# A new precomputed instruction order and engine table for a fused attention and two-MLP kernel

## The chip, the cores and the metric

The kernel runs on one NeuronCore of one Trainium2 chip. The metric is the device time of one execution in microseconds (us). The engines are named as in the profile: PE (TensorE matmul), PEld (TensorE weight load, which overlaps PE), DVE (VectorE), ACT (ScalarE), POOL (GpSimd), SP (SyncE, which issues nearly all the DMAs).

## The reference, cut to what matters

Local attention with block summaries (2 batches, 8 heads, 768 positions, head size 64), and then two MLPs of 512 to 2048 to 512 on the 1536 tokens, all in float32:

```
k_sum = k.reshape(B, H, nb, 32, D).max(axis=3);  v_sum = v.reshape(B, H, nb, 32, D).mean(axis=3)
scores = concat(where(|i-j| < 16, q k^T / 8, -1e9), q k_sum^T / 8 + log 32)
x = softmax(scores) @ concat(v, v_sum)                  # to [1536, 512]
h = x @ w_in1
x = (P(h) / (Q(h) + 1e-6)) @ w_out1    # P cubic, Q = 1 + |b0||h| + |b1|h^2
h = x @ w_in2
out = (h * cos(h)) @ w_out2
```

The weights arrive as 64-bit floats, two 32-bit words for each value.

## The kernel before

Every matrix product is made of float32r matmuls on a high and a low part of each operand (three products: high by high, high by low, low by high). So every weight tile and every activation tile is converted or copied to a high part (`split`, line 757, on ACT, DVE or POOL; the profile shows it at the copy helper's lines L320 for ACT, L325 for DVE and L322 for POOL) and a low part is subtracted from it (`split`, line 759, on POOL or DVE; the profile shows L760). Weights are first rebuilt from their 64-bit form by three integer operations on DVE (`to_f32`, L743, L747, L751).

Attention works on 12 blocks of 128 tokens: scores (`sp`, L624), the mask with a running minimum (L639, DVE), the exponential with its sum (L643, ACT), the sum made safe and inverted (L648 on ACT or L649 on DVE, and L653 on DVE), the scaling of the probabilities (L656, POOL or DVE), their transpose (`ptp`, L670), the product with v (`avp`, L717), and then the high part of x (L320 or L325) and its low part (`xL`, L728, DVE). The first MLP's units follow behind as soon as their tokens are there: `h` (L847), the rational function (L996 to L1024 over ACT, DVE and POOL), and the second product into four PSUM banks (`acc`, L1089). A unit is one slice of 128 of the 2048 hidden columns and one tile of 512 tokens. When the token tile changes, a bank is copied out to SBUF (line 1114, "spill") and the next tile's partial sum is copied into it (line 1098, "reload"); both are copies on ACT (L320) or DVE (L325). The second MLP is made the same way for its first four slices and with a seven-product scheme (L945) for the rest.

Nothing of the order is decided on the chip. `Plan.op` records 2,989 operations with the engines on which each may run and a cost for the planner; `Plan.order` takes them in the order of a table, `ORDER`, which also holds one engine for each operation. The table was made beforehand by a search with replays of a cost model. What the chip runs is one queue for each engine, in that order, and semaphores between the engines. A cost that is of the class `Shared` marks an operation for which the planner reckons with the SBUF port that DVE and POOL share; the class is a float, and nothing on the chip reads it.

`coefficients` (lines 377 to 396) loads the MLP's a and b and makes the scalar sqrt-like coefficient of b from them: on DVE L384, L390, L392 and L395, on ACT L382, L387 and L389, all on 128x1 values.

Of the kernel before, what the change touches and what calls it, by code (L numbers as in the profile page):

```python
# [53 lines left out]


ORDER = (
    "c-rk*+pk>LUH;bkt+nr$*?Z5-p8Ms@nKN^IE<P9EVmq;2J4q7<D>1EO43s7$GBk-2QC9`EC_s_&La0FWfvReu5<;SVAX"
    "X54fd^h%At6-pAM}AI;FVX_ZN?`NLPFw=vo+_OJ!`M^yM5p9TWj0MV}D2}(ex3MEImnQz`3`C4*>*sI48c15oTRr`pyL"
    "P=ohc0o`}Ktt2wLpdrYLQ1S6Vbkclin>ka`K`YAr-UgLs?;8v9a7kDI(mnjeUJ~#v6BfPx;A0_R*6y9W9Wn}_<ke79k3"
    "A8hoHt=&%oYpU7|B)hkHVPpK@-G?op2Lf;?OwV0lrn<rH-7!%rB{|$aN*7Z-@kozvGv)@2f=sdTZi)-=fG!&@dmc`F78"  # L60
    "d2@9ki6<Hnio_y7Lv_ID>=$9VQ9<Bi$3W*g%_98V5^`NQ$}-r)lrjPAaCIoW^3e+lP)XZO&1{s?CemfQPx<xdy?{LIc<"
    "9XWq+zm}Koeg2K;?$5U_K08HoJR3Kg4=2N`SBA|SJA=#3e)GK8x{7jEmlxaZad|vy4KJ3h=H3DN)tOtJ0!6fF=Hq$Z+4"
    "xNPc$|-m7W&OzmbW&Mwr0ylI=)pbP+S|12IbY_@(X?sd82(Ui;mJe6_V%nlg4foU;mmsvmL#jytlX>Ch;%D(!aMcJ=n%"
    "8li=HTcE|f?XX6)kx4$~Zv;L!7x9}`~^vcA4S5C{f8?x(NYUFPwzE{_h&We4XQlGX%64~$f==H2aUOM_Pp`ia&@{>oop"
    "A^lM-l431LCWL@&6|mo6pE*_OB7rne?kxQI5`}=M(;P^N4?)Fvy{KOZ23vryUe|}wq&}o8F04kZEw=%R{xKwza!`#Mq3"
    "|%-mK~|Ugxi&?pJ8--ow9ruK8uO^1b)o-9~n_m}duz-E4E#z~WyPi}YV7S&E+xk@nyCam;!MM;!#WTRoutPyenAl-18<"
    "aR(v?5zg_b4SrU!dG}`V8F=~DO^F+G@r=auGKJt6v;g7PfrLkCf<c_&kfFxD1oyEGCUKFD6FL$I`49}-65{WKCf|=3u="
    "g=`A3uJKj~;)N-UQ+w0)N#Guc~=o@zS4rx4(ypm-Qr)eqVGG9nvCt898g{CW(KKCvAik+XJ3PBfwN3ewTU?g(|cryy_6"
    "jn`#KvDHshoJBMD>LkI1k3%?5d4OHH^^iq#^C7&e;*As)_pfCTyXQGIus3u}8$^q+n3~V>a61GGn!x9_8G)TtdAV~&ME"
    "IM7aESPy!=y{FIOCTFDDuFU+kRPQaV|+6Zp8Sn2FNuDwRj6)^d7QB@VFCMv4hsW>xr+6!$}zb^5qJl_DxSvSdQNzi$3x"  # L70
    "xu{t@cuf3<rSau3Tk=xHKe@B|k^r4ktV2!qO#JM~h^6q_;?@kOCRqdGe9L#otW+YhkM6+D!UpTdZ34igr$)+mldKRkyJ"
    "bWnS=;G&E{VIxp>%UCKg+fg)#lpskT6Ob6B0d-@FqNgH6Mff)pc^L3C@p(i)33(-cfYSFfkG_|Z5U7=Od4H<lP{^hI0e"
    "!RA=igUo;JfWbyN#XsZ!;g$uVX&@qY1=FSAj$XF!m602(f`Lim!YNJo$r!_vk)X#o7829x9b>2vXA5V?AA+`;f|o@;9b"
    "<c$*Xx(B!w2I)AxhQl4RXc1Q6w?kg&WtOF0%WwUy^kOl7Nij?OwijP2Dj@~ZY@lkqcDuY7BqS@XabVIQJ^eYJ2*i=7?u"
    "{@b;Ts+l;o+cYIg=`X+U}O9=M=uMzKf#Y7o3X3_KgYoH(ED47I{Zh`3jX?I;TQhc7ugSePyB`Kim>%(;imXFoNtJ7f{<"
    "heelDROMQ!S|!Xf8@&x_jI)U7q2sup|{GpOF!i{E)WMl|;kGz!Hf|5uozVdo1Z?r%L{<b94d?$Uz?rJx3hSE*0iARf$b"
    "x52J^Uu1H6g^6tROeWZQdWI2i1?PF2d3{wk)|iW>Y_jS3G&?TvR3mNh-l(79AibI)LD*0TrO2r*5eif+Xh5b+RP0S+L6"
    "_A-pCy&Y778cwv)Wg+8phKqibj(zrm}`Fk}F;<qVugrPaGXpdDzZF1k0p2QnvhT2i}qmi}-k;QtWo3x{s{aiqi|}I8GV"
    "~9`@qb(DRXcaWnLWVc-p!*Opxwp(&a#ma6bK30smMzaMj&AQ*AxG0CEuDU~iF>N7v}Bi>{|z|Inr8B;s=oclMpr{)c=u"
    "%WmbU11CAu;VsoY<e`AvXYA3dmX<quQ$83&$5lyvdLL7>=qlWj`R9f+{~)Dm*Oa@o4YZ>f(2zBh;2Vh@^PYCXo4tagD7"  # L80
    "O(B)A;oQglJVhZa0h$)?(}kEwA)2T21lre|1)Su_tQ(&Y;RuMdwE68l7zBJkJvf*v8~EKb-^O^v$fgi7gDab?rnm$LL_"
    ">Ma&tn#kEpseDm}pACcOW*CX*e9+AeAq0tzlAbU1&b?7y3z4xBUQ#uX$*nxa4B0e>??s-^(HVCFDQcwy&9Wuh6g0{_r<"
    "_tG647=nLZu$?_{2Mq9CBC5&DnWNf^AOKNr;WuOzi}NCB%HxjXI$AB_+MyMaZ)B)%J0ziL?|ISk4IPL6Y(Py%>t<%OJo"
    "!Y5H*wk!rtIkcw_y15sKnwxcBiMghsOBCQBFL#`lBn?v^DAo-xnc+J8V3x2m*l_-=DHGXprBxynzByTAN2_A-n0BEY7k"
    "4gxo-TT4kivaYEg-5|AO&8?TCPq^9zoM$fuAy5qR;vZa?A$kS^{`;-oB?kq$8JMnI}$h(fP2q#Zw5y4I^$^dc)uxFrzD"
    "0dhj$J6E@F{JN^9d8`BT~r@P(a`<O^j;P1;Z~vhfCZvE(loH_HK6FevFtDlrg6dW<lP62t{>sBO_>O7NBNL`rS@ez!Xg"
    "mDsDc7)n_*Wf>H$<DeB((l4c_N-xq`5{Nm%nc|b@6AcsxB-KPk*sLf=?junfUlgkFd~~_eLL~#>C2uK`wxP61?C8kVQ?"
    ";e|Y%H)fJVSCxVxjs+j0C3&Tq$2SZ-{m?FPfPsv_{T&GUahBc^CyEsHKpy?x@p79f~S|&vPCkVTz3rRA}l5?fa4oQB!+"
    "JEy^mM)<q_Hj0VM7sE!i8r#5D_!FcKbuC@ghtKJU<V=69v0Kn;Wdi^&S`(I6E|Kl>o{x98~UZ>aTb$Xp%r`PFqdi}q;g"
    "t<tlcVK2e`cA!WGWDAg7wTTUPN}b49jWvv3H4ge^chSLn0n5*dUsUc%os5y!1awDS9YKWlm#=QR@m?6M(7#Jo?fUXkTw"  # L90
    "asR1Mh`X0m%|*K!@0j**#F$}c0gN`TBi+6x`49aWF@B(CS_IITb8Iwa%FB*#c6Njhi!$0TpEQa@Zf(u4Z-#`-n2P<HgN"
    "4ph(9#V}#$<ZUHjhPa8uM6Jj4I%V6`gqRD%xHHpD9Kzh_IQ4gOOEes2nCqD)J7KNs$7H>j{K$qwcoL_{6&g=+0qbA7s&"
    "<<BYZ6f78g+{#)5&7JhD_-UJ4_k$EbU!r8+yJjAvY8<9&{oaKIcl;jjbvsi~$p;FcY`~T_bMcBa6GC8+Q?6Rdrh-H*8="
    "sAUOsa-nt~Y1wjL-254p4;%x$E+K+kduoN+9tf4g%Z7}5A5pzR~45-|83oPwjMRi8jkfEgo*|Gs^KrN``T1J1k{<u<`8"
    "HQ6XXj@Ef-8u@<iH})gCToUiTr4KEqO>N7amL}WKe>DzGTFE-Z&$wc8sVI*b9quvw}jbp*$R>ik?W?i-t{`uEvq8)l?m"
    "=ZGnL?Q34SU?z8c`JN!TY-;kH4I#Avs0t!<`j_of!khKZY#ZE#|%4zw~OOfuXOebonMHW97*)zWswP1E#NBy6`B5}BM$"
    "X2SB@rfOZe8o36Bqk+zn9AK;JTaz~N6*o=Qt$B+KtvR=9YSWu8dP_oKsim2^2FhUSu(!^Q{JSQ!?zk<W3xsRoaX6Tw@F"
    "yJ5;qVi*;0AN2Ij&c=GfuWrt0bA#FlMpiPDEF&;8IzoWRr6E3)f{%NL<sqXt)zr7vGvarfgOvUFmGLYxb|C&q=Z)xGji"
    "lLM>&sn+!NMNw}4t1j0S!YadQOxZTn8|JLbeYk6|0krO;;ML3?BqFOhcR_d`18g86c`-&Yf<`|ufOgJsH_Gz_unPdc3E"
    "4b?yZh2#qXSS8rkXeTuj_|JYS6>{1*-9m}jIPB4w%>$pP|&LPS1Fh!SYz;s9305bG*-ntsU~n`;H!JAb>)f3xTah?WhW"  # L100
    "LgzOuL4m~g`IIvC-K20>3It|W`BDlofGkSn9^O0&`GdaT0MBb;a@Dei1$7pylT+oo<4XX|b1gnYw|h$jN-;CQl;*va<P"
# [1205 lines left out]
```

## Time and profile before

| | |
|---|---|
| median of 3 runs (lowest, highest) | 611.24 us (610.29, 613.06) |
| the profiled execution's own time | 610.86 us |
| its span, first to last instruction | 609.1 us |
| PE, PEld busy | 589.6 us, 498.1 us |
| DVE, ACT, POOL busy | 563.3 us, 426.9 us, 313.6 us |

The profile is of one execution. Its span is 1.76 us under that execution's time and 2.1 us under the median of the runs. Busy times are unions: two instructions of an engine that overlap in the pipeline count once there, while a mean duration of one instruction counts each in full.

### The profile page before, as it was taken

How to read it: one execution, taken by the hardware profiler on the slowest of the kernel's cores; microseconds unless marked ns; L12 is line 12 of the kernel's file. 1: busy time of each engine (PE TensorE's matmuls, PEld its weight loads, DVE VectorE, ACT ScalarE, POOL GpSimd, SP SyncE). 2: the span in 40 equal slices, each digit the busy share in tenths (PEclk: the TensorE clock that was granted, in tenths of full speed). 3: DMA queues.
4: the chain of work that ended last, by engine and by line, in shares of the span. 5: the costliest groups of instructions: out<-in, count | busy, mean ns of one | idle time of the engine just before them, and what ended most of it. 6: DMA issues, size and time to landing. Idle time of an engine off the chain costs nothing.

```text
span 609.1 us, 10750 instructions
## 1 busy us (share of the span) xinstructions
PE 589.6 (97%) x3843; PEld 498.1 (82%) x3843; DVE 563.3 (92%) x1108; ACT 426.9 (70%) x930; POOL 313.6 (51%) x301
## 2 busy tenths in 40 slices
...
GB/s 259 230 238 179 214 186 179 32 0 2 104 49 56 69 70 103 104 35 70 69 70 34 36 69 70 35 70 9 95 105 1 110 63 105 53 19 0 53 36 121
DMA packets 68861, 51.84 MB, mean 85 GB/s; under 512 B 37304, under 2 KB 63160, under 8 KB 68808
## 3 DMA queue, kind: packets, MB, share of 16 engines
...
q8 instruction: 30, 0.49, 0.3%
...
## 4 chain that ended last, share of the span: by engine, by line
PE 54%; DVE 36%; issue 4%; ACT 3%; POOL 1%; DMA 1%; DVEq 0%; ACTq 0%; POOLq 0%
PE acc L1089 25%; PE h L945 15%; PE h L847 9%; DVE h L1021 4%; DVE tu L1018 3%; DVE f L747 3%; DVE te L1024 3%; DVE f L751 3%; DVE te L1008 3%; DVE f L743 3%; DVE te L1010 3%; DVE sc L639 2%; DVE gl L760 2%; PE ktp L461 1%; PE avp L717 1%
## 5 line engine op out<-in xcount | busy, mean ns | idle before, releaser
L1089 PE MATMUL acc<-gh,w 128*128 128x512 f32 (+1 forms) x416 | 123.1, 378 | 1.9 <-ACT acc L320 1.2
L1089 PE MATMUL acc<-w,gh 128*128 128x512 f32 x382 | 119.2, 393 | 0.8 <-ACT room L320 0.8
L847 PE MATMUL h<-xH,w 128*128 128x512 f32 (+1 forms) x352 | 111.4, 374 | 0.7 <-DVE big L493 0.7
L1089 PEld LDWEIGHTS acc<-gh,w 128*128 128x128 f32 x416 | 75.2, 188 | 19.2 <-ACT acc L320 2.6
L760 POOL TENSOR_TENSOR gl<-te,gh 128x512 fp32r<-128x512 f32 (+1 forms) x48 | 63.3, 1320 | 52.3 <-DVE gh L325 27.3
L760 POOL TENSOR_TENSOR w<-f,w 128x512 fp32r<-128x512 f32 x48 | 66.7, 1391 | 39.6 <-ACT w L320 27.1
L1006 POOL TENSOR_TENSOR tu<-tu,tf 128x512 f32<-128x512 f32 (+1 forms) x46 | 59.6, 1296 | 40.7 <-ACT tf L998 38.9
L1089 PE MATMUL acc<-gl,w 128*128 128x512 f32 (+1 forms) x208 | 78.0, 375 | 0.0
L1089 PEld LDWEIGHTS acc<-w,gh 128*128 128x128 f32 x382 | 67.3, 189 | 11.3 <-ACT room L320 1.2
L847 PEld LDWEIGHTS h<-xH,w 128*128 128x128 f32 x352 | 64.5, 188 | 12.8 <-DVE big L493 0.9
L1089 PE MATMUL acc<-w,gl 128*128 128x512 f32 x191 | 74.3, 389 | 0.0
L847 PE MATMUL h<-xL,w 128*128 128x512 f32 (+1 forms) x176 | 65.2, 371 | 1.2 <-DVE xL L728 1.2
L847 PE MATMUL h<-big,w 128*128 128x512 f32 x240 | 59.0, 391 | 0.1
L847 PEld LDWEIGHTS h<-big,w 128*128 128x128 f32 x240 | 44.7, 188 | 11.0 <-DVE te L1024 1.3
L747 DVE SCALAR_TENSOR_TENSOR f<-raw,f 128x512 int32<-128x512 int32 x64 | 50.7, 794 | 0.3
L751 DVE SCALAR_TENSOR_TENSOR f<-raw,f 128x512 int32<-128x512 int32 x64 | 49.0, 767 | 0.2
L1016 ACT ACTIVATE h<-tf 128x512 f32<-128x512 f32 (+1 forms) x52 | 29.6, 568 | 25.2 <-DVE te L1010 23.2
L1047 ACT ACTIVATE h<-h 128x512 f32<-128x512 f32 x48 | 28.0, 583 | 26.6 <-DVE h L1044 24.3
L1089 PEld LDWEIGHTS acc<-gl,w 128*128 128x128 f32 x208 | 39.1, 188 | 8.0 <-DVE gl L760 0.9
L1013 ACT ACTIVATE tf<-tu 128x512 f32<-128x512 f32 (+1 forms) x52 | 31.4, 604 | 17.5 <-POOL tu L1006 15.3
L1089 PEld LDWEIGHTS acc<-w,gl 128*128 128x128 f32 x191 | 35.9, 188 | 7.9
L643 ACT ACTIVATE sc<-sc,mn 128x120 f32<-128x120 f32 x96 | 37.1, 389 | 6.4 <-DVE mn L639 6.2
...
## 6 DMA issues: line engine op xcount, KB each, us to landing
...
```

The costliest lines, as they stand in the source:

```text
L643: lambda e, pr=pr, hh=hh, sv=sv: nc.scalar.activation(out=sv()[:, pr, :], in_=sv()[:, pr, :], func=ACTF.Exp, scale=-1.0, bias=mn.t[:, hh, ...
L747: lambda e: nc.vector.scalar_tensor_tensor(out=ft.t.bitcast(I32), in0=lohi()[1], scalar=-0x40000000, in1=ft.t.bitcast(I32), op0=ALU.bitwis ...
L751: lambda e: nc.vector.scalar_tensor_tensor(out=ft.t.bitcast(I32), in0=lohi()[0], scalar=29, in1=ft.t.bitcast(I32), op0=ALU.logical_shift_r ...
L760: lambda e: E[e].tensor_tensor(out=lo(), in0=x(), in1=hi().bitcast(F32), op=ALU.subtract),
L847: nc.tensor.matmul(out=h.t[:, 0:n], lhsT=lt, rhs=rt[:, kk, cs], start=(k0 == 0 and i == 0), stop=(k0 == 2 and i == 5))
L945: nc.tensor.matmul(out=bank.t[:, c], lhsT=lt, rhs=rt, start=start and i == 0, stop=stop and i == 5, skip_group_check=True)
L1006: lambda e: E[e].tensor_tensor(out=U(), in0=U(), in1=Z(), op=ALU.add))
L1013: lambda e: nc.scalar.activation(out=Z(), in_=U(), func=ACTF.Ln, bias=QC))
L1016: lambda e: nc.scalar.activation(out=H(), in_=Z(), func=ACTF.Exp, scale=-1.0))
L1021: lambda e: nc.vector.scalar_tensor_tensor(out=H(), in0=U(), scalar=2.0, in1=H(), op0=ALU.subtract, op1=ALU.mult, reverse0=True))
L1047: lambda e: nc.scalar.activation(out=H(), in_=H(), func=ACTF.Abs))
L1089: nc.tensor.matmul(out=dst, lhsT=lt, rhs=rt, start=(un.start and not have and i == 0), stop=(un.stop and i == 2), skip_group_check=have)
```

## The change

The `ORDER` table is another one, and three of the four DVE operations of `coefficients` get a planner cost of the class `Shared`. The operations themselves, their tiles and their number stay.

```diff
 ORDER = (
-    "c-rk*+pk>LUH;bkt+nr$*?Z5-p8Ms@nKN^IE<P9EVmq;2J4q7<D>1EO43s7$GBk-2QC9`EC_s_&La0FWfvReu5<;SVAX"
...
+    "c-rk)+mED2bw5?7>bqaMze``fzD@V^^i0pCcRV|L@p^5~nzfg)*S3V$2HUcTu`#SkSm(k;$bcU}0*r`+M8rdau!L}ADT"
...
 )
...
-        P.op([("V", 0.1)], [], [co_r],
+        P.op([("V", Shared(0.1))], [], [co_r],
              lambda e: nc.vector.tensor_scalar(out=co[:, 8:9], in0=co[:, 7:8], scalar1=1e-30, scalar2=None,
                                                op0=ALU.max))
...
-        P.op([("V", 0.1)], [], [co_r],
+        P.op([("V", Shared(0.1))], [], [co_r],
              lambda e: nc.vector.scalar_tensor_tensor(out=co[:, 9:10], in0=co[:, 9:10], scalar=co[:, 7:8],
                                                       in1=co[:, 8:9], op0=ALU.mult, op1=ALU.add))
...
-        P.op([("V", 0.1)], [], [co_r],
+        P.op([("V", Shared(0.1))], [], [co_r],
              lambda e: nc.vector.tensor_scalar(out=co[:, 8:9], in0=co[:, 9:10], scalar1=0.5, scalar2=None,
                                                op0=ALU.mult))
```

The table is base85 text over zlib: for each of the 2,989 places the index of the next operation among those left, in two bytes, and one byte for its engine. Both tables decoded and laid beside the list of operations say what moves. 256 operations change their engine:

| from, to | operations | which, mostly |
|---|---|---|
| DVE to POOL | 59 | low parts (29), high parts (10), weight sums (8), the sum of Q(h) (6), scaling of probabilities (5) |
| POOL to DVE | 43 | low parts (26), high parts (8), the sum of Q(h) (4) |
| DVE to ACT | 59 | copies out of the product scheme's banks (19), high parts (15), spills (6), reloads (4) |
| ACT to DVE | 49 | the same kinds: 12, 9, 5 and 8 |
| ACT to POOL, POOL to ACT | 23 and 23 | high parts (22 and 22) |

DVE ends with 986 operations (1,012 before), ACT with 842 (832), POOL with 285 (269); PE keeps 735 and SP 141. In every queue the order changes too, by a few places at a time: the longest run of operations that both tables have in the same order is 437 of 735 on PE, 643 on DVE, 533 on ACT, 177 on POOL and 99 of 141 on SP. PE's first 36 operations (through the transposes of block 5's q, 38 us in the profile) keep their order. DVE's queue around the coefficient operations, with one name for each operation:

```
before: ... xL(block 0), co L384, L747, mask, L743, mask, L751, co L390, cast, L747, co L392, co L395, xL(block 1), L653, L751 ...
after:  ... xL(block 0), L747, co L384, L751, L743, cast, L747, co L390, xL(block 1), mask, co L392, L653, co L395, L751 ...
```

At the change of the token tile in slices 8 to 11 of the first MLP, the reload of bank 0 moves from DVE to ACT (tile 1), and PE's queue has other work between the last product of the old tile and the first of the new one (H is a half of a unit's `h`, 1.36 us; O one bank of a unit's second product, 0.68 us; f the slice, T the tile, d the bank):

```
tile 0 to 1, before: ... O(f11 T0 d0) d1 d2 d3, H, H, O(f8 T1 d0), H, O(f8 T1 d1) ...
             after:  ... O(f11 T0 d0) d2 d1 d3, H, H, O(f8 T1 d1), H, H, H, H, H, O(f8 T1 d3), O(f9 T1 d3), O(f8 T1 d0) ...
tile 1 to 2, before: ... O(f11 T1 d3), H, H, H, O(f8 T2 d2) d1 d3 d0 ...
             after:  ... O(f11 T1 d2), H, O(f11 T1 d1), H, O(f8 T2 d3), H, H, O(f9 T2 d3), H, O(f8 T2 d1) d0 ...
```

In the table's common order, 28 of PE's operations from about 100 us on (5 before) have no other PE operation between them and the last DVE, ACT or POOL operation that they depend on.

At the end, between the last unit's Sin (L1049) and the end, PE's queue holds 11 operations where it held 12.

## Rows read from the trace of the kernel before

**Rows 1.** The page's first part: busy time, share of the span, instructions.
```profile
PE 589.6 (97%) x3843; PEld 498.1 (82%) x3843; DVE 563.3 (92%) x1108; ACT 426.9 (70%) x930; POOL 313.6 (51%) x301
```
**Rows 2.** Busy time by stage: stretch, its length, each engine, clock, DMA.
```profile
0.00:120.00 120.00, 106.92 (x1346) 88.36 (x1347) 109.30 (x382) 97.50 (x332) 76.08 (x102) 1.00 0.71 192
120.00:200.00 80.00, 80.00 (x385) 66.07 (x384) 75.34 (x115) 55.71 (x94) 50.16 (x43) 1.00 0.15 45
200.00:300.00 100.00, 98.12 (x428) 79.52 (x427) 97.84 (x146) 69.72 (x120) 65.17 (x52) 1.00 0.22 70
300.00:400.00 100.00, 99.08 (x431) 79.96 (x430) 97.36 (x150) 77.37 (x138) 55.79 (x46) 1.00 0.17 53
400.00:600.00 200.00, 200.00 (x1236) 179.97 (x1235) 181.98 (x317) 125.07 (x246) 66.39 (x60) 1.00 0.18 59
600.00:609.10 9.10, 5.44 (x27) 4.27 (x25) 1.45 (x3) 1.55 (x3) 0.00 (x0) 0.92 0.31 115
```
**Rows 3.** PE's timeline, 0 to 60 us: start, length, instruction, idle time before.
```profile
1.42 3.78 PE L354 MATMUL warm<-ident 128*128 128x128 f32 x16 [1.42 <-POOL ident masks.py:199]
...
21.35 0.65 PE L670 MATMUL ptp<-ident,sc 128*120 128x128 f32 x4 [1.47 <-POOL sc L656]
...
29.75 1.15 PE L624 MATMUL sp<-room,qT 64*64 64x120 f32 x32 [1.80 <-ACT qT L320]
...
32.41 0.39 PE L847 MATMUL h<-xL,w 128*128 128x256 f32 x1 [1.20 <-DVE xL L728]
...
40.56 0.66 PE L575 MATMUL qtp<-ident,qk 128*128 128x128 f32 x4 [1.68 <-DVE te L1024]
```
**Rows 4.** DVE's timeline, 27 to 33 us.
```profile
27.28 0.14 DVE L384 TENSOR_SCALAR co<-co 128x1 f32<-128x1 f32 x1
27.34 0.68 DVE L747 SCALAR_TENSOR_TENSOR f<-raw,f 128x512 int32<-128x512 int32 x1
27.94 0.27 DVE L639 CUSTOM_DVE_ANT_0 sc<-sp,room 128x120 f32<-128x120 f32 x1
...
30.34 1.23 DVE L392 SCALAR_TENSOR_TENSOR co<-co 128x1 f32<-128x1 f32 x1
31.61 0.15 DVE L395 TENSOR_SCALAR co<-co 128x1 f32<-128x1 f32 x1
31.68 0.68 DVE L728 TENSOR_TENSOR xL<-avp,xH 128x512 fp32r<-128x512 f32 x1
```
**Rows 5.** POOL's timeline of the same stretch.
```profile
29.90 1.65 POOL L760 TENSOR_TENSOR w<-f,w 128x512 fp32r<-128x512 f32 x1 [3.83 <-DVE w L325]
```
**Rows 6.** ACT's timeline, 27 to 30 us.
```profile
27.45 0.20 ACT L387 ACTIVATE co<-co 128x1 f32<-128x1 f32 x1 [0.52 <-DVE co L384]
27.69 0.20 ACT L389 ACTIVATE co<-co 128x1 f32<-128x1 f32 x1
...
29.11 0.59 ACT L320 COPY qT<-qtp 128x512 f32<-128x512 f32 x1
```
**Rows 7.** PE's waits over the span: total us, times, longest; the banks' three.
```profile
PE acc L1089 <- ACT acc L320: 1.2, 2, 1.0
...
PE acc L1089 <- ACT room L320: 0.8, 1, 0.8
...
PE acc L1089 <- DVE acc L325: 0.6, 1, 0.6
```
**Rows 8.** Groups by line and shape: busy us, mean ns of one.
```profile
L760 POOL TENSOR_TENSOR gl<-te,gh 128x512 fp32r<-128x512 f32 x41 | 56.3, 1376 | 52.2 <-DVE gh L325 27.3 <-ACT gh L320 19.8 <-PE h L945 2.3
...
L760 DVE TENSOR_TENSOR gl<-te,gh 128x512 fp32r<-128x512 f32 x33 | 24.4, 740 | 0.9 <-ACT gh L320 0.6
...
L656 POOL TENSOR_TENSOR sc<-sc,su 128x480 f32<-128x480 f32 x16 | 16.5, 1036 | 12.0 <-DVE su L653 10.2 <-ACT h L1016 1.6 <-PE h L847 0.2
...
L809 DVE TENSOR_TENSOR f<-f 128x256 f32<-128x256 f32 x15 | 7.1, 486 | 0.1
...
L656 DVE TENSOR_TENSOR sc<-sc,su 128x480 f32<-128x480 f32 x8 | 6.8, 848 | 0.1
...
L325 DVE COPY tu<-h 128x256 f32<-128x256 f32 x13 | 5.4, 419 | 1.6 <-PE h L945 1.5
```
**Rows 9.** The three weight lines on DVE: duration ns min/median/max, one line each.
```profile
L743 DVE TENSOR_SCALAR f<-raw x64: 397/421/1536, 21.0 to 547.4; 128x512 int32<-128x512 int32 x64
```
```profile
L747 DVE SCALAR_TENSOR_TENSOR f<-raw,f x64: 670/685/1782, 21.6 to 549.5; 128x512 int32<-128x512 int32 x64
```
```profile
L751 DVE SCALAR_TENSOR_TENSOR f<-raw,f x64: 661/686/1662, 22.3 to 555.9; 128x512 int32<-128x512 int32 x64
```
**Rows 10.** The same three as groups: busy us, mean ns.
```profile
L747 DVE SCALAR_TENSOR_TENSOR f<-raw,f 128x512 int32<-128x512 int32 x64 | 50.7, 794 | 0.3
L751 DVE SCALAR_TENSOR_TENSOR f<-raw,f 128x512 int32<-128x512 int32 x64 | 49.0, 767 | 0.2
L743 DVE TENSOR_SCALAR f<-raw 128x512 int32<-128x512 int32 x64 | 38.8, 611 | 0.8 <-DMA raw<-in_moe_w_out_dram 0.6 <-DMA raw<-in_moe_w_in_dram 0.2
```

More of the change, by code (lines that the diff above doesn't have):

```diff
@@ L56 @@
 ORDER = (
-    "c-rk*+pk>LUH;bkt+nr$*?Z5-p8Ms@nKN^IE<P9EVmq;2J4q7<D>1EO43s7$GBk-2QC9`EC_s_&La0FWfvReu5<;SVAX"
[L58 to L101, printed above, removed]
@@ L102 @@
-    "L-<rhLHJa;Pway13CxV1bQ?MSG~HyHc8!x*b+S9y*g0;39^p=!$Z3;f8K)IF;naIgd*-B*R?SbA3F}a;6La!hP2-NZ>$"
-    "X`fwmArLJRqEKNA83{?sP;JQnGQ8Jw~ppbi$tP8Iyr|ZVz_Okwe_TEo?xB2>KV<la|oD(8rhm0%SWEVg"
+    "c-rk)+mED2bw5?7>bqaMze``fzD@V^^i0pCcRV|L@p^5~nzfg)*S3V$2HUcTu`#SkSm(k;$bcU}0*r`+M8rdau!L}ADT"
+    ")IEBm@WvA;F8IC=&lcgv28+dCfUh)ypH1@|dZ;Oix$UsdM?A-#Jwf`zb<E2LN%6z7K%ez7U?EPap$%FqR-D^!Z_!zVgX"
+    "wzY9{vanoFQMz${(Q4}CbsOrhhmZn8Q_fj$XR&-MpSq4pm^qsy>`ALEoJx`F(tq5RWDS#hLVF7zmek}i{(&g@kgi(?Bk"
+    "Y!n?RZl_GswmR56({eHZ`>eN{^hSoMIn@0tpFZ<R9?A!4Nl~8`QXKm!Nn)9z;B;;0FEzhU-`~=-+yEI$YQa8^mu+=Zo="
@@ new lines @@
+    "Wt?DA?gd-&ni!CNrje)WxC?5Y*~<F{YmnM^h(v&rn6(+Q8&o6kRe|Iy*SM;D)b91=Kq;`9yg{Ql9=?)!fCI}dJYy}hfK"
+    "(Us@tAA0WDd*>gi>szxKDSGFqsvbRj=z;M>T`jMSPVOtqWmEQ{C_0_X#bk2fLOq_;ono-M=do2)!MV6w?7~f`v#gjeim"
+    "W~9Wbck9{r>JztIT?RsMGoWEQM#Py2^&*VbQ*N)o-<X-AiyW`ao7?+36vqt5&psaP6ZX)q7#|VzP5>nIy^EpL{Mnj$x*"
+    "j)9G~Idwg=Rnt6LWWB;?C26*V9_dPWCC#MfI58k<{KT(ve+aJ%ofzn>_sX`qdCUID3^);nNRk5|Db@0X))i=7iQb7;}b"
+    "+45r>a}X%xBe}PvrJvDuBU)Xi7P0RzYP52%aI(*FdF<t^aT}$f&ZCat0kY=4nx@<5=c7Yc0Akk$;mq(5$BJFJ3EMTHJz"
@@ new lines @@
+    "$4_Fqw7`truh!@+<+0sVtgJPjXw>JO0b{`G6soub&v7ck#Cm+iuIwv+8_&ws!5@Bg*2k=>@%zlr`kYNl}v;p1I^8hY>b"
+    "pf0s;(IAk3ydVKWfO2)?k^cm5-*2_H9|l;clLzM>;FXBL9MZ^0PtOC92oXV&T!5Gcp$#$5MW*MQ=jpJGLq;>~`M%chbE"
+    "P)vm!JGZ{8+&L{tw~$58r*4d;%hR=bd+G#)l`r_dSy75unG}Xfy()Pn4=io$WS2z}a$onou^-`Go8i=%tsXN%9)pQ8Ca"
+    "_qSR#tigP7xx0CTU(wBT_@32RMK9pNs&-Xl!(xhE_poIvg)4_!ZL-;lLO_OFqP05IIgy1!h_sAL{mI-C_)>hfhTQCg9V"
+    ";m*E-(cSZ-}l?)l<mvYflj)l6m2fkQCSBBgD4sf$zk#<cY?snGg-(aQGhS>h3G`FFP{F8@C#5+X&UNfHY}(l1ptvXPh-"
@@ new lines @@
+    "4%OAN)OkBi`Z5Zq{*U`5)L3&eJjD^xH_&&wbl#UaH60+9>Gp-%E#1t}zx3HD=uA6eeEuTgAX--@LaVmwY~voz({Ao`)-"
+    "mXMTXRqoMLgo`}CfLKvfLAQj+gD%XN<pN(1MqZd^nq3)1lc@9vDJ}nBQ=&g9>$<Lf6_UX3XTtNO3cK)atSTWmaF{gz+`"
+    "KIZ0B^ntoz8Bzw+Oyi3xL_@zg4griq#ZB(}+*}6D*e<fY+7M3es$he~TDH@b#eT+`9FutQmMb#9$B!cn-Q1VaNA;4Np+"
+    "$gU*M;<_56)>s`N)MV^yK;W3H@gyg>7IXF4dC57s~r<9tPc>$<n25PrCgk1<iW?(&&sZ{BuQJSSuRAIy+`J*mm)*?!!p"
+    "bW@HZ!+=0^T?<^?b*tri4gGKdu;}D=BrApstO}k^=JC0|1r{$ZhoZ0Fe=NSttaiaAH4ncFPp3(qSWx#TMXPeqE=K0enI"
@@ new lines @@
+    "sDv40*!(CdxIbR@tVtV2?1xHOlH5~@FO68pW|w{KTi79IqUk!xOj@r4((P|dTl@B66r^B-pKYK)@3h-hD@^BC)X<HdYD"
+    "4)pk1Hqzq$B;Fi|t5J=3yb5=PXuP5*=~O*C!8U9i9kpbW^z)|4Wak`tHoh!l1|3kYsX&w^1<@DcRV0%~h>Zxxq0Ib};H"
+    "L8Vd=-XD)Nutc(3^u`6ifqnFin+L)b&M0e3w&U>=46a8eC|@SN$Bk*{mGjE0ScMz~*4k?#11-)hxI2w2Y^Pf~p0t5asO"
+    "UdA1YAK>*&cP3cIcMcr;u07c;|Qm0xTUrS;o@m@)@q;ynus!CF+Ov1jT@1nXUuLOb0q)aqOqFH%zGVz4g!v{pP94LX)&"
+    "h(y(LTnyV<Z;!eAw<8{^~T0TJX-CfWw|H|)$R6@UNXt^BoW8$qYmT;aa2X^HV6>JYOSq=D0Hwv^wnZ~1~I{IP?eX$<Gy"
@@ new lines @@
+    "zUelM>y1*XtPM>(mF5EIn4f?%<j{rwR95GKO+hnm6y*r6suwU%uqKMSc~EQI4=7%;}empkCqoet$}yYRHn>=ZAOXtsIt"
+    "=1nS7iy0_y=zZ#uN5IpwMt3!0U90ApKn^dJK}iC|@^ftgi#%K<NxYkGP+AioGe;|h11e)!b|^*358R_rRf8yuA_)QI?9"
+    "3O0HcF`d{i6m&J(o%pn}}jW-de(PM-$))2-6Pu_th-4Db!U8SDlvW4nRR<o43>S+_`f!89~^R-3bLMNqWV2+#5;C{w4!"
+    "z7JzgsW%OO*ygAX|Ml!<1cI+u3^9_VlsaR4+m1SjJt%z5v7NPO)RGPK^=Cu^=aKVToUvxcq=^rZS_KLo47xz4?3q?Nj<"
+    "Lxb?2MxG@*Mrm3$(T-&vOlE5yW+AG-Hu?=pqk+C?NbxR<tWzMFq=^=B3h8wK~QFm#QhD|#iH(#Wt6pT;$7U^OVcz@DWC"
```

20 lines of the change are left out of this document (added).

## The prediction

> **What bounds the kernel now.** I read the page's busy times first, because they say how much any reordering can give: PE is busy for 589.6 of 609.1 us [rows 1], and neither table adds or removes a matmul. A new order can only win back PE's idle time, 19.5 us, or add to it. So the second view is where that idle time lies. By stage [rows 2], PE's idle time is 13.1 us up to 120 us, nothing from 120 to 200, 1.9 from 200 to 300, 0.9 from 300 to 400, nothing from 400 to 600, and 3.7 behind 600, where the last product drains through a copy and a DMA. 280 of the 609 us have no idle PE at all, and the granted clock there is 1.00, so the order can't gain anything in them. It can only lose there.
>
> The third view is PE's timeline in the early stage, which names the gaps [rows 3]. The reader is to see that they are few and large: 1.47 us for a scaling on POOL, 1.80 for a copied qT, 1.20 for the low part of x, 1.68 for a bank that DVE's L1024 holds, besides the 1.42 before the first matmul, which no table touches. These five are 7.6 of the 13.1; the rest are small ones. DVE is behind most of them: it is busy for 109.3 of the first 120 us, and for 97 to 98% between 200 and 400 us [rows 2], though PE itself has little idle time there. The fourth view, PE's waits, gives the idle time in the middle: 2.6 us in four waits for banks, two of them for reloads on ACT, one for a reload on DVE, one for a spill on ACT [rows 7].
>
> **The change, part by part.** The Shared marks are read by the planner only. On the chip they cost 0, and no cover is needed for that, since they put no instruction in any queue. Everything else is the table.
>
> Engines. DVE gives away 118 operations and takes 92, 26 fewer. Priced each by the mean of its own kind in the trace, those that leave sum to 70.6 us and those that come to 55.2, so DVE is relieved by 15.4 us; that is 0.59 us for each of the 26, which lies between a 256-wide copy at 0.42 or a weight sum at 0.49 and a low part at 0.74 or a scaling at 0.85 [rows 8]. POOL takes 82 and gives 66; by the same means it gets 16.7 us more, as one low part costs 1.38 us there against 0.74 on DVE [rows 8]. ACT gets 5.8 us more. POOL is 51% busy and ACT 70% [rows 1], so by total both have room. The relief of DVE is 3.1 us before 120 us, 0.6 from 120 to 200, 5.6 from 200 to 400 and 6.1 after 400. The last part meets a PE without idle time and gives nothing. The middle part can give at most the 2.8 us of idle time there, the first at most its 3.1.
>
> The early gaps. The gap of 1.20 us is PE waiting for xL of block 1, at 31.68 on DVE. In front of it stand L392 for 1.23 us and L395 for 0.15, both on 128x1 values [rows 4]. L392 lasts until POOL's low part of a weight, 29.90 to 31.55, is through [rows 5]; the other one-column operations here take 0.14 to 0.15 us, so 1.1 us of it is waiting. The Trainium skill, page "SBUF — State Buffer", section "Who interferes with whom", says that a DVE instruction with two SBUF inputs and a POOL instruction that reads SBUF exclude each other for the whole instruction; the row agrees with it. In the new queue xL stands ahead of L392 and L395, and one of its inputs is PSUM, as in the row where it takes 0.68 us. So this gap closes: -1.2 us. The price is just before it: L384 now has a second weight operation, L747, ahead of it, 0.60 us from start to start [rows 4]. ACT's L387 already waits 0.52 us for L384, and behind it in ACT's queue stand L389, a copy and then the qT copy at 29.11 [rows 6], for which PE waits 1.80 us. So that gap grows by 0.6 us. What is late next is the score product of block 3, and behind it the first `h`. Sum of the two: -0.6 us. The 1.47 us gap also gets shorter, since the v mean's copy no longer stands between the two operations on the sums, but PE then only waits longer for the same qT; I count 0, and -0.5 as the bound. For the remaining early gaps the queues change by single places, and I find no sign: 0, with bounds of -3.1 (DVE's relief there, in full) and +2 (a gap the size of those in rows 3 opening anew).
>
> The reloads. In both tile changes of slices 8 to 11 PE's queue now has more between the last product of the old tile and the first on the same bank. For bank 0 of tile 1 five halves and two banks' products stand between it and the place where it was, and its reload moves from DVE to ACT; this wait of 0.6 us goes. For tile 2 three halves and an O follow the first new product, so the two waits on ACT, 1.2 us, go as well: -1.8 us. The spill's wait of 0.8 us [rows 7] I keep: between that spill and the next product on its bank PE has 3.4 us of work in either table. Bound: 0 where the other banks, which come up sooner than before, wait in their stead, -2.8 where all idle time of the middle goes.
>
> The transfers. SP's queue changes by a few places, among the first loads too; PE's first products use the same set of k and q tiles in the same order, and the first 120 us have DMA at 0.71 of its engines [rows 2], so I put 0 on it, with +0.5 as the bound for a late q tile.
>
> The end. After the last unit's Sin PE has 11 operations where it had 12, one bank's product less (0.68 us) to hide DVE's last three operations. Two halves of that are an even guess: +0.3, bounds 0 and 0.7.
>
> DVE's waits for POOL. The three weight lines have medians of 421, 685 and 686 ns [rows 9] and means of 611, 794 and 767 [rows 10]; 64 times the differences is 12.2, 7.0 and 5.2, together 24 us that DVE stood waiting beside 313.6 us of POOL, or 0.08 us per us. POOL's 16.7 us more would then cost DVE 1.3 us, out of a relief of 15.4. It is hidden by that relief: 0. Without that cover it is +1.3.
>
> Sum: -0.6 -1.8 +0.3 = -2.1 us on the profiled execution's 610.86. That execution lies 0.4 us under the median of the three runs, 611.24, so I predict 609.1. About 0.5%, or 3.1 us, is what a measurement of this kernel can tell from no change, so the likeliest answer is: not told apart from before, on the fast side.
>
> **The rivals.**
> - Faster: DVE's relief reaches PE. For it: DVE is nearly never idle between 20 and 400 us, and PE's gaps trace back to it. Then the early stage gives the 3.1 us and the 1.1 us of L392's waiting, the middle its 2.8: 7.0, less 0.3 at the end, some 604.5. Against it: in the early stage the gaps come from single operations in the wrong place, and a few us of load spread over 120 don't move those. It decides if PE's idle time up to 120 us falls below 10 us.
> - Slower: low parts that come late from POOL. 29 of them go there, and each is ready 0.64 us later than on DVE, or later still behind POOL's own queue; the third product of each O needs it. Place: 200 to 600 us, where PE runs without gaps. For it: PE's rows there show no slack, and in the new table 28 of PE's operations have their producer right ahead of them, against 5. By the Trainium skill's rule above a POOL operation can hold DVE for its whole length, and by that alone the 16.7 us would eat the relief; the weight lines show 0.08 of it. Against it: POOL is idle half the time. If 10 of the 29 land on PE's path with 0.64 us each, it is +6.4 on top of the sum, 615.5; it decides from about eight on (5.2 us, from 609.1 to 614.3).
> - Slower by the early stage: the L384 chain is worse than its 0.6 us, or a q tile lands late, and the blocks behind it shift: +2 to +4, without the reloads' gain 613 to 615.
> - The change does nothing: the marks are inert, and the moves cancel. It ends at 611, inside the forecast's class.
>
> **How the numbers follow.** The forecast, with the rival of no effect in it, has 0.42; DVE's relief reaching PE 0.33; the late low parts 0.16; the early stage 0.09. So faster by over 0.5% is 0.33, within 0.5% 0.42, slower 0.25. The forecast's own range is 607 to 612. The range goes to 604 on the fast side, the first rival's 604.5 with half a us, and to 616 on the slow side, where it holds the early stage's case and most of the late low parts; about one in ten is left out on each side.
>
> **What would show it.** In the changed profile: L392 no longer ahead of L728 and the wait of `h` for xL gone; the wait of `sp` for qT near 2.4 us; no PE wait for a reload between 240 and 280 us; PE's idle time 200 to 400 near 1 us; DVE's busy time 12 to 15 us lower and POOL's 15 to 18 higher; 120 to 200 and 400 to 600 still without idle PE. I am wrong if PE's waits name POOL's L760 by more than 2 us in total, or if the early idle time differs from 12.5 by more than 2.5.

## The result and the profile after

The changed kernel takes 602.1 us (601.5 to 603.2, 4 runs) against 611.0 us for the kernel before: a ratio of 0.985, with a 95% interval of 0.982 to 0.988. That is 8.8 us faster, where 2.1 were forecast, and below the range's 604. The profiled execution's span is 599.4 us, 9.7 less than before. Lines of the changed file stand two further down (L392 of before is L394); in runs whose table takes one line less in the file they stand one higher (L1088 for L1089).

The page's busy times, to hold against [rows 1]:

```profile
PE 586.1 (98%) x3843; PEld 499.7 (83%) x3843; DVE 547.9 (91%) x1082; ACT 434.2 (72%) x940; POOL 331.8 (55%) x317
```

DVE is 15.4 us lighter, POOL 18.2 heavier and ACT 7.3; the engine table's sums had been 15.4, 16.7 and 5.8. PE runs the same 3,843 matmuls, and its busy time falls by 3.5 us all the same. So busy time is not the time that PE needs, and that is what the prediction's largest error hangs on (below).

Busy time by stage of the changed kernel, in the columns of [rows 2]:

```profile
0.00:120.00 120.00, 110.45 (x1373) 91.51 (x1375) 106.68 (x386) 98.38 (x331) 78.97 (x106) 0.99 0.72 192
120.00:200.00 80.00, 80.00 (x378) 66.32 (x375) 74.18 (x114) 58.38 (x100) 50.39 (x43) 1.00 0.16 49
200.00:300.00 100.00, 100.00 (x443) 82.84 (x442) 95.76 (x149) 74.37 (x127) 68.13 (x56) 1.00 0.24 77
300.00:400.00 100.00, 100.00 (x451) 83.18 (x450) 97.40 (x148) 82.80 (x147) 57.80 (x46) 1.00 0.15 49
400.00:590.00 190.00, 190.00 (x1184) 171.42 (x1183) 171.75 (x286) 119.27 (x236) 76.51 (x67) 1.00 0.18 59
```

From 200 to 300 us PE runs 443 matmuls where it ran 428, though its busy time rises by 1.9 us only. To see where the time is won, I cut both traces where the same number of matmuls has run. First the kernel before (stretch, length, PE busy with the count of matmuls, clock, DMA):

```profile
0.00:48.00 48.00, 38.66 (x587) 1.00 0.88 242
0.00:98.00 98.00, 84.92 (x1137) 1.00 0.80 216
0.00:200.00 200.00, 186.92 (x1729) 1.00 0.49 133
0.00:400.00 400.00, 384.12 (x2584) 1.00 0.34 98
0.00:600.00 600.00, 584.12 (x3818) 1.00 0.29 85
```

and the changed kernel:

```profile
0.00:47.40 47.40, 39.26 (x588) 0.96 0.90 242
0.00:94.60 94.60, 85.05 (x1137) 0.98 0.84 224
0.00:196.50 196.50, 186.95 (x1729) 0.99 0.50 136
0.00:390.30 390.30, 380.75 (x2584) 1.00 0.35 100
0.00:590.20 590.20, 580.65 (x3817) 1.00 0.29 86
```

The lead is 0.6 us after 588 matmuls, 3.4 after 1,137, 3.5 after 1,729, 9.7 after 2,584 and 9.8 near the end. So the gain is made in two places: 2.8 us between 48 and 98 us, and 6.2 us between 200 and 400 us. Nothing is won or lost from 98 to 200 and from 400 on. Up to 48 us the two are not told apart (the granted clock was 0.96 there in the changed run and 1.00 before; see the end).

DVE's busy time, cut at the same counts, tells more than its total. From 1,729 to 2,584 matmuls (columns as in [rows 2]), the kernel before and the changed one:

```profile
200.10:400.10 200.00, 197.20 (x856) 159.47 (x855) 195.20 (x296) 147.09 (x257) 120.86 (x97) 1.00 0.20 62
196.60:390.40 193.80, 193.80 (x857) 160.53 (x856) 186.97 (x286) 151.43 (x262) 122.88 (x100) 1.00 0.20 63
```

For the same work of PE, DVE is busy for 8.2 us less, not the 5.6 of the prediction. The three weight lines, with the same number of operations, are behind a good part of it; over the whole run of the changed kernel, against [rows 10]:

```profile
L749 DVE SCALAR_TENSOR_TENSOR f<-raw,f 128x512 int32<-128x512 int32 x64 | 51.1, 800 | 0.4
L753 DVE SCALAR_TENSOR_TENSOR f<-raw,f 128x512 int32<-128x512 int32 x64 | 47.5, 746 | 0.4
L745 DVE TENSOR_SCALAR f<-raw 128x512 int32<-128x512 int32 x64 | 31.7, 502 | 1.4 <-DMA raw<-in_moe_w_in_dram 1.0 <-POOL w L762 0.5
```

Above their medians (687, 685 and 421 ns) that is 16 us, where it was 24 us before, though POOL has more to do. Between 1,729 and 2,584 matmuls it is 7.4 us against 12.4.

PE's waits from 120 to 595 us, four in the kernel before [rows 7], are none in the changed one. The two early places on which the prediction had dwelt, first PE's timeline of the changed kernel:

```profile
30.03 1.15 PE L626 MATMUL sp<-room,qT 64*64 64x120 f32 x32 [0.70 <-ACT qT L322]
31.11 0.38 PE L849 MATMUL h<-xH,w 128*128 128x256 f32 x1
31.34 0.28 PE L849 MATMUL h<-xL,w 128*128 128x256 f32 x1
```

and DVE's:

```profile
29.53 0.69 DVE L730 TENSOR_TENSOR xL<-avp,xH 128x512 fp32r<-128x512 f32 x1
...
30.33 0.21 DVE L394 SCALAR_TENSOR_TENSOR co<-co 128x1 f32<-128x1 f32 x1
```

The wait of `h` for xL is gone, and the coefficient operation that had stood 1.23 us [rows 4] takes 0.21 behind it.

### The profile page after: what moved, and what is told of

It is laid out like the page before. It is cut to its first block, busy times and chain, and to the rows that moved or that the text cites. A ratio compares the mean times of both kernels' runs of the same rounds, so it can differ in the third digit from the quotient of the medians.

```text
span 599.4 us, 10768 instructions
## 1 busy us (share of the span) xinstructions
PE 586.1 (98%) x3843; PEld 499.7 (83%) x3843; DVE 547.9 (91%) x1082; ACT 434.2 (72%) x940; POOL 331.8 (55%) x317
## 4 chain that ended last, share of the span: by engine, by line
PE 89%; DVE 6%; SPq 2%; DMA 1%; ACT 1%; issue 0%; DVEq 0%
PE acc L1091 44%; PE h L849 26%; PE h L947 15%; PE avp L719 1%; PE ptp L672 1%; DMA raw<-in_moe_w_in_dram 1%; PE sp L626 1%; DVE sc L641 1%; DVE f L749 1%; SPq L507 1%; SPq L454 1%; DVE f L753 1%; PE vmp L542 0%; PE qtp L577 0%; DVE f L745 0%
## 5 line engine op out<-in xcount | busy, mean ns | idle before, releaser
L849 PE MATMUL h<-xH,w 128*128 128x512 f32 (+1 forms) x352 | 110.0, 373 | 0.3 <-DVE big L495 0.3
L762 POOL TENSOR_TENSOR gl<-te,gh 128x512 fp32r<-128x512 f32 (+1 forms) x57 | 75.8, 1331 | 47.7 <-ACT gh L322 27.1
L762 POOL TENSOR_TENSOR w<-f,w 128x512 fp32r<-128x512 f32 x47 | 66.3, 1412 | 31.5 <-ACT w L322 25.5
L1008 POOL TENSOR_TENSOR tu<-tu,tf 128x512 f32<-128x512 f32 (+1 forms) x48 | 61.7, 1286 | 32.6 <-ACT tf L1000 31.8
L849 PEld LDWEIGHTS h<-xH,w 128*128 128x128 f32 x352 | 64.5, 188 | 12.4 <-DVE big L495 0.5
L324 POOL TENSOR_SCALAR gh<-te 128x512 fp32r<-128x512 f32 (+1 forms) x26 | 18.9, 728 | 51.0 <-DVE te L1054 20.2
L1049 ACT ACTIVATE h<-h 128x512 f32<-128x512 f32 x48 | 27.9, 582 | 20.7 <-DVE h L1046 20.3
L998 ACT ACTIVATE tu<-h,co 128x512 f32<-128x512 f32 (+1 forms) x52 | 33.6, 651 | 10.9 <-PE h L849 10.8
```

Of the source, the lines that this page charges most:

```text
L324: nc.gpsimd.tensor_scalar(out=o, in0=i, scalar1=1.0, scalar2=1.0, op0=ALU.mult, op1=ALU.mult)
L762: lambda e: E[e].tensor_tensor(out=lo(), in0=x(), in1=hi().bitcast(F32), op=ALU.subtract),
L849: nc.tensor.matmul(out=h.t[:, 0:n], lhsT=lt, rhs=rt[:, kk, cs], start=(k0 == 0 and i == 0), stop=(k0 == 2 and i == 5))
L998: lambda e: nc.scalar.activation(out=U(), in_=H(), func=ACTF.Square, scale=b1s))
L1008: lambda e: E[e].tensor_tensor(out=U(), in0=U(), in1=Z(), op=ALU.add))
L1049: lambda e: nc.scalar.activation(out=H(), in_=H(), func=ACTF.Abs))
```

## The experiments

Every ratio is to the kernel before, run on the same chip beside it, and is one of means; a gain in us by the ratio can differ by some 0.8 us from that of the medians. The changed kernel was not run beside e10, e15 and e17: its 602.1 us is that of the result. Where a table is spliced or edited, it was decoded, reordered so that every operation still follows those that it depends on, and coded again; the diffs say in short what was done to the decoded table.

**Which stretch carries the gain (e1, e2).**

```diff
-order = old
+order = new[:867] + [op for op in old if op not in new[:867]]     # e1, engines likewise
+order = old[:861] + [op for op in new if op not in old[:861]]     # e2, engines likewise
```

> Part of the change alone: order and engines of the new table for the operations that the new table places in the first 110 us of PE work (867 of 2,989), order and engines of the old table for all that is left. In the changed profile PE is 3.5 us ahead after 100 us of its work and 9.7 us at the end. Theory A (PE's gain is made where PE loses its waits, and kept): only the early 3.5 us, so 607.5 us, and PE's late starts at the first MLP's changes of token tile, 200 to 400 us, cost their 6 us as before. Rival B (the early part takes load from DVE, and the later waits for banks and reloads go because DVE is less behind): the middle's waits shrink too, 602 to 605 us. Rival C (the early part is worth nothing by itself, since PE later catches up with DVE anyway): 610 to 611 us.

> The complement: old table for the operations that it places in the first 110 us of PE work (861), new table for the rest. Theory A: the 6.2 us of the middle stay, 604.8 us, with no PE wait for a reload between 200 and 400 us. Rival B: part of the middle's gain goes, 606 to 609 us. Rival C: all of the gain stays, 602 us.

e1: 608.5 us, ratio 0.995 (0.994 to 0.997), or 2.9 us of the gain (2.7 by the medians). e2: 606.3 us, 0.991 (0.988 to 0.993), or 5.7 us (4.9). Together that is 8.6 of the 9.1 us that the change's own ratio gives, by the medians 7.6 of 8.8. The traces are sharper: from 1,729 to 2,584 matmuls e2 takes 193.8 us like the changed kernel, and e1 199.9, where the kernel before takes 200.0. In e1's trace PE's waits behind 120 us are the old ones to 0.1 us:

```profile
PE acc L1088 <- ACT acc L319: 1.2, 2, 1.0
PE acc L1088 <- ACT room L319: 0.8, 1, 0.8
PE acc L1088 <- DVE acc L324: 0.5, 1, 0.5
```

In e2's trace there is no wait of PE behind 120 us. So the two parts are independent, as theory A had it; a head start of the early part is passed on and does not mend the middle.

**Order or engines (e3, e4).**

```diff
-order, engine = old, old
+order, engine = new, old     # e3
+order, engine = old, new     # e4
```

> Order of the new table, but every operation on the engine that the old table gives it (the 256 moves undone). If the order carries the gain (what PE has between the last product of an old tile and the first on the same bank of a new one, and which operation DVE does first), 602 to 605 us. If the engines carry it (DVE 15 us lighter), 609 to 612 us. If the two are made for each other and each queue has operations in the wrong place without the other, slower than 611 us.

> Order of the old table, engines of the new one (the 256 moves alone). If the engines carry the gain, 602 to 605 us; if the order does, 609 to 612 us; if the two are made for each other, slower than 611 us.

e3: 684.1 us, ratio 1.119 (1.116 to 1.122). e4: 632.5 us, 1.034 (1.032 to 1.037). Neither carries the gain alone; the two are made for each other. In e4, with the new engines in the old order, the three weight lines stand 34 us above their medians (16 in the changed kernel, 24 before): what the moves take off DVE goes into these longer operations. In e3 PE waits again and again for single operations that come late in a queue laid out for another load:

```profile
PE h L847 <- DVE te L1024: 8.4, 7, 2.8
PE acc L1089 <- POOL gl L760: 6.8, 9, 1.2
PE acc L1089 <- DVE gl L760: 5.4, 4, 2.7
```

**PE's queue or the others, in the middle (e5, e6, e7).**

```diff
-PE queue 229..439: old
+PE queue 229..439: new       # e5, all other queues old; e6: the new table with these places old
```
```diff
 PE queue, old table (e7)
-H, O(f8 T1 d0), H, O(f8 T1 d1)
+H, H, O(f8 T1 d1), O(f8 T1 d0)
...
-O(f8 T2 d0), H
+H, O(f8 T2 d0)
...
-O(l1 f0 T1 d2), H
+H, O(l1 f0 T1 d2)
```

> The old table with one queue changed: PE's operations 229 to 439 (200 to 396 us, the stretch in which the changed kernel gained 6.2 us) in the order of the new table. All engines and all other queues as before. Theory A1 (PE loses its time there because its next operation waits while others are ready; PE's own order carries the gain): 605 to 606 us, PE without waits between 200 and 400 us. Rival A2 (the copies and conversions on the other engines come earlier in the new table; PE's order only fits them): no gain, 611 us, or slower, as PE then meets products whose operands the old queues make later.

> The mirror image: the new table, but PE's operations 229 to 439 in the order of the old one. Theory A1: the 6.2 us come back, 608 us. Rival A2: about 602 us, since the other queues still deliver early. If both are needed: slower than 608 us.

> The old table with three moves in PE's queue and nothing else: the product of slice 8 on bank 0 of tile 1 goes behind the one on bank 1 (PE stopped before it at 244.5 us), the one on bank 0 of tile 2 behind the next half of h (stop at 273.2), and the second MLP's first product on bank 2 of tile 1 behind the next half of h (stop at 383.6). The starts of the matmuls show 1.0, 1.3 and 1.1 us lost at these three. Theory A1: 3.4 us less, 607.6 us. Rival A2: what goes in front is not ready either, or the copy is later still: under 1 us, 610 to 611.

e5: 621.5 us, ratio 1.017 (1.014 to 1.019). e6: 618.4 us, 1.012 (1.009 to 1.014). e7: 610.7 us, 1.000 (0.998 to 1.002). Theory A1, which I had held, falls: PE's order alone does not win the time. e7 shows why. The waits for reloads fall from 1.8 us to 0.2, and new ones open; all of PE's waits behind 120 us in e7:

```profile
PE h L846 <- DVE te L1023: 0.7, 1, 0.7
PE h L846 <- DVE te L1051: 0.6, 1, 0.6
PE acc L1088 <- DVE gl L759: 0.5, 1, 0.5
PE acc L1088 <- ACT acc L319: 0.2, 1, 0.2
```

1.8 us of new waits, all on DVE. What PE does not lose before a reload or a spill, it loses at the next thing that DVE delivers: its trace takes 199.6 us from 1,729 to 2,584 matmuls, 0.4 less than before.

**The coefficient operations (e8).**

```diff
 DVE queue, old table
-co L390, cast, L747, co L392, co L395, xL(block 1), L653
+co L390, cast, L747, xL(block 1), co L392, L653, co L395
```

> The old table with two moves in DVE's queue and nothing else: the second and the third of the coefficient operations marked Shared (L392, L395) go behind the low part of x of block 1, as in the new table. The wait of 1.2 us of h for that low part goes in any case. Theory A (gaps of PE are local and what is won stays won): 1 us less, 610 us. Rival (DVE is full up to 75 us, so the gap opens again at the next thing that PE needs of it): no difference, 611 us, and PE's next waits longer by as much.

610.8 us, ratio 1.000 (0.998 to 1.002). The wait for xL is gone from its trace, PE's wait for the scaling of the probabilities on POOL from 25 to 48 us is 1.4 us (1.0 before), and nothing is left at the end: after 588 matmuls both traces stand at 48.1 us. The second theory again: a closed gap reopens further on.

**DVE's pace in the middle (e9, e10, e12, e13).** Here work is left out or doubled; no queue is reordered, but that e12 has e7's three moves as well.

```diff
+SOME = {983, 1188, 1244, 1281, 1505, 1542, 1573, 1808}   # eight L747, 172 to 336 us
 for o in order:
+    if o.seq in SOME: continue          # e9, e12
     o.fn(o.eng)
+    if o.seq in SOME: o.fn(o.eng)       # e10, e13
```

> The old table, and 8 of the weight operations L747 left out, those at 172, 190, 208, 232, 243, 278, 308 and 336 us (the middle word of these weights is then missing from the result): 8 times 0.68 us, 5.4 us less for DVE between 170 and 340 us, and no queue in another order. Theory D (in the first MLP DVE delivers only just as fast as PE takes, so each us of DVE work less is up to a us less in which PE stops; the new table's 5.6 us of DVE work less there are its 6.2 us): PE's stops between 200 and 400 us nearly vanish, 605 to 606 us. Rival Q (each stop comes from one operation in the wrong place of one queue, and a lighter DVE doesn't move it): 609 to 611 us, the stops at 244, 273 and 384 us still there.

> The mirror image: the new table, and the same 8 weight operations issued twice each (the second gives the same bits), 5.4 us more for DVE in that stretch. Theory D: the stops come back, 606 to 608 us. Rival Q: the new queues have their distance, PE stays without waits, 602 to 603 us.

> The old table with both: the three moves in PE's queue (alone: 0) and the 8 weight operations L747 left out between 172 and 336 us (alone: 2.7 us less; the middle word of these weights is then missing). Theory DQ (two kinds of stops: those before reloads and spills come from the queues' order, the others from DVE's pace, and closing one kind alone lets PE run into the other): 605 us, close to the 6.2 us of the new table. If the parts only add up: 608 us.

> The old table with the same 8 weight operations issued twice, 5.4 us more of DVE work between 172 and 336 us, which cost the new table 11 us. Theory DQ (PE is paced by DVE there under either table): 617 to 622 us. If the old table has more room in its queues than the new one: under 616 us. If the new table's slack is what it was searched for: the old one loses more than 11 us, over 622 us.

e9: 607.9 us, 0.996 (0.994 to 0.998), 2.4 us less. e10: 613.4 us, 11.3 above the changed kernel's 602.1. e12: 609.0 us, 0.997 (0.995 to 0.999), so the moves add nothing that the times show to e9, and its theory falls (by the traces e12 gains 3.4 us from 1,729 to 2,584 matmuls, of which it loses 0.3 again behind, and e9 2.9). e13: 615.7 us, 1.008 (1.006 to 1.010), 5.1 us more. In e9 the waits at 273 and 383 us, for copies on ACT, stay, and the one for DVE's reload is gone:

```profile
PE acc L1089 <- ACT acc L320: 1.2, 2, 1.0
PE acc L1089 <- ACT room L320: 0.6, 1, 0.6
```

In e10 PE waits for DVE first of all:

```profile
PE h L849 <- DVE te L1026: 3.0, 4, 1.1
PE acc L1091 <- POOL gl L762: 1.3, 2, 0.9
PE acc L1091 <- DVE gl L762: 0.9, 2, 0.5
```

So 5.4 us of DVE work are worth about half when taken away under the old table, their whole when added there, and twice themselves when added to the new one. Counted by what DVE was busy the three come nearer to each other. From 1,729 to 2,584 matmuls, e9, e13 and e10:

```profile
202.30:399.40 197.10, 195.23 (x857) 160.03 (x856) 191.68 (x289) 147.37 (x256) 118.81 (x97) 1.00 0.19 62
199.80:404.70 204.90, 198.33 (x856) 159.09 (x855) 200.39 (x302) 147.73 (x258) 122.80 (x98) 1.00 0.19 62
198.70:402.10 203.40, 197.52 (x856) 159.62 (x855) 196.92 (x295) 152.50 (x264) 125.97 (x101) 1.00 0.20 62
```

In e9 only six of the eight operations lie in the stretch: DVE is busy for 3.5 us less there and the stretch is 2.9 shorter. In e13 it is 5.2 more and 4.9 longer, in e10 9.9 more than in the changed kernel and 9.6 longer. The stretch goes with DVE's busy time, 0.8 to 1.0 us for each us, and DVE idles for 4.5 to 6.8 us in all five. Where the two tables' engines or queues are mixed over the whole stretch, it idles for 9.6 us and more there (e3 to e6).

**The early part (e11, e14, e16, e17).**

```diff
+SOME = {163, 175, 193, 199}          # e11, left out: L747 at 27, 36, 46, 61 us
+SOME = {193, 187, 199, 211, 205}     # e16 left out, e17 twice: L747 at 46 to 73 us
+order = old to 27 us of PE work, new to 66 us, old behind     # e14, engines likewise
```

> The old table, and 4 weight operations L747 left out, those at 27, 36, 46 and 61 us (again the middle word of four weight tiles is missing): 2.7 us less for DVE early, the same size as the new table's relief of 3.1 us before 120 us. If the early gaps of PE are paced by DVE: 2.7 us less, 608.2 us, kept to the end. If they come from chains through ACT, POOL and the loads: 610 to 611 us.

> Order and engines of the new table only between 27 and 66 us of PE work (about 48 to 98 us of time), the old table before and behind. In the profiles the two tables' first 27 us of PE work differ by less than executions of one table do, and 2.3 us are won behind. If the early gain is made there: 608 to 609 us. If the first loads and copies carry it: 610 to 611 us.

> The old table, and the five weight operations L747 at 46, 54, 61, 67 and 73 us left out (the middle word of these five weight tiles is then missing): about 3.9 us less for DVE inside the stretch in which the new table wins 2.3 us. If DVE's pace makes PE's gaps there: 608 to 609 us. If the queues' order makes them: 610 to 611 us, the gaps still there.

> The mirror image: the new table, the same five operations issued twice, 3.4 us more for DVE in that stretch. If DVE's pace makes PE's gaps there: 605 us or more. If not: 602 to 603 us.

e11: 610.2 us, 0.999 (0.998 to 1.001); no trace shows where PE waited in it. e14: 608.3 us, 0.997 (0.995 to 0.999), so 2.0 to 2.3 us of the early gain are made in its stretch, which for PE's queue is 43 to 90 us in the profile of before. Only 9 operations change their engine in e14, and DVE has one fewer, which points to the order for most of what it wins. e16: 609.9 us, 0.999 (0.998 to 1.001), a gain of 0.4 us by the ratio that can be anything from -0.4 to 1.3. e17: 606.9 us, 4.8 above the changed kernel, a heavier DVE costing the new table more than the 3.4 us that it adds. The traces tell e16 from before. From 506 to 1,137 matmuls, the kernel before, the changed one, e14 and e16:

```profile
42.90:98.00 55.10, 51.20 (x634) 43.11 (x633) 54.02 (x206) 50.14 (x183) 38.09 (x42) 1.00 0.74 193
42.20:94.60 52.40, 50.54 (x634) 42.74 (x633) 50.86 (x207) 49.19 (x182) 40.82 (x45) 1.00 0.76 203
43.90:97.60 53.70, 50.68 (x633) 42.76 (x632) 52.38 (x207) 50.48 (x186) 38.19 (x42) 1.00 0.75 198
41.80:95.70 53.90, 50.83 (x636) 42.92 (x635) 52.14 (x202) 49.92 (x182) 36.69 (x42) 1.00 0.75 197
```

The five other runs with the old table there and the clock at 1.00 (e2, e5, e8, e12, e13) take 55.1 to 55.2 us, so these differences are well beyond the scatter. A lighter DVE alone wins 1.2 of the 2.7 us, and e14 1.4. Again the stretch goes with DVE's busy time, 1.9 us less in e16, 1.6 in e14 and 3.2 in the changed kernel. PE's waits from 48 to 98 us add up to 2.8 us in six in e16, 3.8 in eight in the kernel before and 1.3 in three in the changed one; all name DVE or ACT, none a load.

**A candidate (e15).**

```diff
 SP queue, new table
-raw(f0 w_in), vw(block 1, half 0), ...
+vw(block 0, half 0), raw(f0 w_in), ...
```

> A candidate: the new table, and in SP's queue the v rows of block 0's first half (vw, L707) go ahead of the first weight load; nothing else moves. In the changed profile they are issued at 17.9 us, behind the broadcast loads of the coefficients, which hold SP for 1.5 and 2.1 us, and PE waits 0.9 us for them at 23.2. If PE's early waits can be closed one by one: 601.2 us. If the next wait takes the time (as with the coefficient operations): 602 us.

601.6 us, ratio 0.986 (0.983 to 0.988), not told apart from the changed kernel's 0.985. No version here beats it.

## Why the prediction was wrong

The side was right (0.33 for faster, 0.25 for slower), but the most likely answer, 0.42, was no difference that a measurement tells, and the size was wrong. By its own sign it was wrong too: PE's idle time up to 120 us is 9.55 us, more than 2.5 from the 12.5 and below the 10 that were to decide for the fast rival. By its steps:

- **The bound of the middle, "at most the 2.8 us of idle time there", is the step that failed,** and with it the 1.8 us that the sum took from there for waits at the banks. PE lost 6.2 us there. Idle time is counted from a matmul's modelled end, and a stop costs more. The largest one, in PE's timeline of the kernel before:

```profile
273.19 0.39 PE L1089 MATMUL acc<-gl,w 128*128 128x512 f32 x1
274.58 0.73 PE L1089 MATMUL acc<-gh,w 128*128 128x512 f32 x2 [1.01 <-ACT acc L320]
275.15 0.39 PE L1089 MATMUL acc<-gl,w 128*128 128x512 f32 x1
```

  The idle time shown is 1.01 us. Matmuls of this shape start every 0.227 us here when nothing stops them (the median over the trace), and from 273.19 to 274.58 there are 1.39: 1.16 lost. The next two then take 0.73 where such a pair takes 0.61: 0.12 more. Small stops don't show as idle time at all, since the next matmul starts before the last one's modelled end. Summed over all starts from 200 to 400 us, what exceeds the median of each shape is 5.9 us in the kernel before and -0.3 in the changed one, the 6.2 (3.0 in e9, 5.5 in e7). The sentence that "280 of the 609 us have no idle PE" rests on the same view, but holds: from 120 to 200 and from 400 on nothing was won.
- **The reloads, -1.8 us.** The waits went, with the spill's 0.8 that I had kept. A longer distance in PE's queue does close them (e7), but that wins 0.4 us in the stretch and nothing by time: PE then waits for DVE.
- **DVE's relief, not in the sum.** It was left to the fast rival, and that is the term that the middle was made of. In e9, e13 and e10 the stretch from 200 to 400 us goes with DVE's busy time; the changed kernel has 8.2 us less of it there, which at e9's 2.9 us for 3.5 is more than the 6.2 that PE had to lose (an estimate: no run took the whole 8.2 off the old table). It is larger than the 5.6 of the moved operations because the three weight lines stand 5.0 us less above their medians there (DVE's durations sum to 10.6 us less; busy time counts overlaps once). The engines alone don't give this: in e4 DVE's busy time in the stretch is 195.4 us, as before. Which places of which queue keep DVE from waiting is not taken apart further: the three edits of PE's queue that I tried gave nothing or a loss.
- **DVE's waits for POOL, +1.3 hidden.** By the same reading, durations above the medians of the weight lines, they did not grow with POOL's work but fell, from 24 us to 16. That the total relief came out at 15.4 us as summed is in part luck: it holds this fall, which I had not counted.
- **The early stage, 0 for the remaining gaps.** Wrong by 2.8 us in the profile, by 2.3 in e14. Of the two gaps that I worked out, xL's closed as I said (-1.2); qT's copy ended at 29.98 us where it had ended at 29.70, 0.3 later and not 0.6, and PE waited 0.70 us for it where I had said 2.4. Closing the first was worth nothing by e8: I should have seen that DVE, busy for 109 of 120 us [rows 2], only hands the gap on. Of the 2.7 us between 43 and 98 us, 1.2 come with a lighter DVE (e16) and 1.4 with the new table on most of that stretch (e14). How far the two are the same gain, and what wins the rest, stays open.
- **The end, +0.3.** It was 0 to 0.1 us: the lead near 600 us is that of 400 us.
- **The rivals.** The fast one, DVE's relief reaching PE, is nearest in time, 604.5, and its mechanism is what e9, e10, e13 and e16 show. That its sum came so near is in part luck: it had 4.2 us early, where 2.8 were won, and was held to 2.8 in the middle, where it was 6.2. The low parts that come late from POOL did not happen: no PE wait names L762 behind 120 us. They do once the load grows (e10).
